# One written-out list of instructions in another order, on a kernel that runs attention and a feed-forward block on one core

## The chip, the cores and the metric

The kernel runs on one core of one Trainium2 chip. The metric is the device time of one execution in microseconds (us); lower is better. The engines are TensorE (PE, matmuls), VectorE (DVE), ScalarE (ACT), GpSimd (POOL) and SyncE (SP, which issues almost all transfers).

## The reference, cut to what matters

```
q, k, v: 8 batches x 8 heads x 576 rows x 64
q_s = softmax of q over its 64 columns;  k_s = softmax of k over its 576 rows
kv = k_s^T v  (64 x 64 per head);  x = q_s kv, laid out as 4608 tokens x 512
h = x @ w_in  (512 x 2048);  g = relu(h)^2;  out = g @ w_out  (2048 x 512)
```

The weights arrive as 64-bit floats (512 KB for each chunk of 128 hidden columns of w_in, and the same for w_out) and are taken apart into a high and a low fp32r half on the chip.

## The kernel before

**Blocks and words.** The tokens are worked in nine blocks: blocks 0 to 7 hold 512 tokens of one batch each, block 8 the 64 left over from every batch. A pair is two heads; a batch has four pairs. Every product of the feed-forward block is three fp32r matmuls (high x high, high x low, low x high).

The program is one text, `ORDER`, a list of 3969 words. Each word stands for the next step of one unit of work, and almost every step has instructions on a single engine. The loop at the end of the kernel walks the list once and emits each word's instructions; so the list fixes, for every engine, the order of its queue. Nothing reorders it later: an engine runs its own words strictly in the order of the list and waits wherever an input is not there yet.

**Words of the first phase** (pairs 0 to 7, block 0, and the weights). `Lq`, `Lk`, `Lv` load parts (a, b, ...) of q, k, v for a pair (all from SP's queue, but `Lk0b`, `Lq0b`, `Lq1a` and `Lq1b` from ACT's); `Wi`, `Wo` load a weight chunk. For a weight chunk: `wl` and `wt` (ACT) and `wc`, `wd` (DVE) build the fp32 value, through the fourth PSUM bank, `wh` (ACT) rounds it to the high half and `wp` (POOL) makes the low half. For a pair: `m`, `qm` (DVE maxima), `T`, `S` (PE, through which the largest k is spread), `mc`, `ks` (DVE), `ke`, `qe` (ACT, exponentials), `qs`, `qn` (POOL, subtract and scale q), `sm`, `rc` (DVE) with `sa` (POOL) between them, `vc` (POOL, copies v into place), `KV` (PE), `rs`, `kn` (scale kv), `TA`, `TB` (PE, turn q), `ca`, `cb` (ACT), `PX`, `PL` (PE, q times kv), `xh`, `xl` (split x). Block 0: `H` (PE, x times w_in), `r`, `sq`, `gh`, `gl`, `O` (PE). `Z` is a matmul of zeros on PE that computes nothing: a filler.

**Words of the later phase** have a colon and the number of the instance. `h1`, `r1`, `sq1`, `gh1`, `gl1`, `o0_1` to `o3_1` are block 1. From block 2 on two chunks of 128 hidden columns are made at a time by seven quarter products in place of eight: `B11`, `T1`, `T2`, `B21`, `B22`, `T3`, `T4`, each six matmuls of 256 columns, n = 0 to 55 counting the pairs of chunks over blocks 2 to 8. Between them stand short steps on the same PSUM banks: `seed` (ACT copies a bank after B11; T2 needs it), `e5` (ACT, after T1; B22 needs the bank), `u2` (ACT, after T2; T3 needs the bank), `a1` (DVE adds, after B22), `b1` (DVE adds, after T3; T4 needs the bank). Then `ra`/`rb`, `sqa`/`sqb`, `gha`/`ghb` (ACT) and `gla`/`glb` (DVE) make the squared activations, and `o0` to `o7` (PE, three matmuls of 512 columns each) multiply them with w_out; `away` stores a finished block.

The attention of later pairs runs beside it: `load_k`, `load_q`, `load_v` (SP), `k_max`, `k_less`, `k_bound`, `k_spread`, `q_max`, `q_less`, `q_sum`, `q_norm`, `q_turn` (DVE), `k_exp`, `q_exp`, `q_high`, `parts` (ACT), `q_low` (POOL), `kv` (PE and then DVE), `low0`, `low1`, `high` (PE, then ACT and DVE). `wo` and `s34` (SP) bring w_out and sums of w_in back from memory into rings of three tiles; `words`, `sums`, `s_high`, `s_low`, `ct..`, `cT..`, `cB..` prepare combinations.

**The two rings.** Passing tiles live in a ring of four (tag `raw`: sums, turned q, stored rows) and a ring of three (tag `w`: weight values; later three spare tiles). A new tile takes the place that has been held longest, and waits until its last user is done.

```
    with tc.manual_schedule():
        for token in ORDER:
            if ":" not in token:
                first_token(token)
                continue
            if token not in running:
                running[token] = units[token]()
            if isgenerator(running[token]):
                next(running[token], None)
```

Of the kernel before, what the change touches and what calls it, by code (L numbers as in the profile page):

```python
# [51 lines left out]
sm2 PL0@C0 Z PX0@B2 lf0 wli0 wci0 xh0 xl0 Z Z Z Z Z TB1@C0 T2@C1 mc2 Z Z Z TA1@B2 S2 cb1 wli1 KV1@C0 sa2 rc2 qn2 vc3
wdi0 ca1 wti1 ks2 rs1 wci1 Z TB2@C1 whi0 kn1 Lv2b Lk3b wpi0 Z Z PX1@C0 ke2 cb2 H0.0@B0 vc2 KV2@C1 TA2@B2 qm3 qs3 wdi1
xh1 whi1 wpi1 Lk3a Wi2 Lv4b m3 Wi3 Wo2 Wo3 Wi4 Lk4b Lq4b Lk5b Lq5b Lv5b Lq4a Wo0 Lk5a xl1 H0.1 rs2 kn2 wli2 wti2 ca2
PL1@B2 qe3 PL2@C1 lf2 lf1 wli3 wci2 PX2@C0 sm3 xh2 wdi2 sa3 rc3 qn3 xl2 H1.0@B1 T3@B2 H1.1 H1.2 mc3 wti3 whi2 wci3 wdi3
S3 TB3@C0 wpi2 H2.0@C2 H2.1 H2.2 wlo2 wlo3 ks3 wto2 whi3 wco2 wdo2 ke3 wpi3 wli4 wto3 cb3 KV3@B2 TA3@C1 rs3 kn3 who2
# [1105 lines left out]
```

## Time and profile before

| | before |
|---|---|
| three timed runs | 855.24, 855.8, 858.2 us; median 855.8 us |
| the profiled execution, its time | 855.73 us |
| its span, first to last instruction | 853.9 us |
| PE busy | 841.1 us (98% of the span) |
| DVE, ACT busy | 543.5 and 542.5 us (64% each) |
| POOL busy | 278.5 us (33%) |
| chain that ended last | PE 86%, DVE 4%, DMA 3%, ACT 3% |

The span is what the trace covers; 1.8 us of the execution's time lie around it. A busy time is the time in which at least one instruction of the engine is shown at work; for PE the ends of matmuls are modelled, and neighbours overlap, so busy does not mean that nothing is lost. The chain is followed back from the last instruction to whatever released it.

### The profile page before, as it was taken

Reading aid. Unit: us, or ns where it says so; the run is one execution under the profiler, and the core shown is the slowest. Engines: PE = TensorE matmul, PEld = TensorE weight load, DVE = VectorE, ACT = ScalarE, POOL = GpSimd, SP = SyncE. Lnnn points to the kernel's source line nnn. Section 1 sums busy time; section 2 is a strip of 40 time slices with the busy share of each in tenths; the row PEclk is TensorE's granted clock in tenths of the full one; section 3 lists DMA queues with packets and bytes.
Section 4 is the critical chain, followed back from the end, with each engine's and each line's share of the span. In section 5 each row is a group of like instructions: output and inputs, shape, how many; then the busy total and the mean of one; then the engine's idle time right before and its main releaser. Section 6 shows DMA issues by size and latency. Waiting matters only on the chain.

```text
span 853.9 us, 15149 instructions
## 1 busy us (share of the span) xinstructions
PE 841.1 (98%) x5377; PEld 735.7 (86%) x5377; DVE 543.5 (64%) x1077; ACT 542.5 (64%) x1102; POOL 278.5 (33%) x233
## 2 busy tenths in 40 slices
PE   8999999999999999999999999999999999999997
PEld 7688778888889898988988889888889898998996
DVE  7888878979896868577586768576843322322111
ACT  4998855567676776667666766677566544544433
POOL 4786842756534450222213221224112300210000
PEclk9999999999999999999999999999999999999999
DMA  9999745763886769666667487776846174443451
GB/s 219 288 311 269 221 127 171 254 213 94 255 247 177 229 188 280 197 222 186 196 184 251 141 217 233 222 213 168 238 126 230 37 242 145 161 157 127 141 180 50
DMA packets 121003, 166.68 MB, mean 195 GB/s; under 512 B 47584, under 2 KB 88544, under 8 KB 120928
## 3 DMA queue, kind: packets, MB, share of 16 engines
q1 hardware_dynamic: 120272, 165.03, 63.9%
q8 instruction: 42, 0.69, 0.4%
q10 hardware_dynamic: 656, 0.69, 0.3%
q14 instruction: 33, 0.27, 0.1%
HBM read 134.48 MB, written 31.20 MB: 194 GB/s over the span
## 4 chain that ended last, share of the span: by engine, by line
PE 86%; DVE 4%; DMA 3%; ACT 3%; SPq 2%; issue 1%; ACTq 0%; POOL 0%; DVEq 0%; POOLq 0%
PE bank L1076 30%; PE o_ps L727 14%; PE o_ps L729 14%; PE o_ps L728 14%; PE bank L710 3%; PE bank L712 3%; PE bank L711 3%; PE bank L695 2%; PE bank L622 1%; DMA wo<-out_kept 1%; DMA raw_i<-in_moe_w_in_dram 1%; DVE g_lo L721 1%; DMA qt<-in_q_dram 1%; DMA vt<-in_v_dram 0%; SPq L383 0%
## 5 line engine op out<-in xcount | busy, mean ns | idle before, releaser
L727 PE MATMUL o_ps<-wo,g_hi 128*128 128x512 f32 x576 | 228.0, 396 | 2.0 <-ACT g_hi L716 1.4
L729 PE MATMUL o_ps<-wo,g_lo 128*128 128x512 f32 x576 | 225.2, 391 | 0.2 <-DVE g_lo L721 0.2
L728 PE MATMUL o_ps<-wo,g_hi 128*128 128x512 f32 x576 | 224.9, 390 | 0.0
L721 DVE TENSOR_TENSOR g_lo<-r,g_hi 128x512 fp32r<-128x512 f32 x128 | 94.5, 741 | 105.4 <-ACT g_hi L716 104.8
L729 PEld LDWEIGHTS o_ps<-wo,g_lo 128*128 128x128 f32 x576 | 108.1, 188 | 25.3 <-DVE g_lo L721 1.4
L727 PEld LDWEIGHTS o_ps<-wo,g_hi 128*128 128x128 f32 x576 | 108.4, 188 | 23.0 <-ACT g_hi L716 1.8
L1037 ACT ACTIVATE r<-bank 128x512 f32<-128x512 f32 x128 | 76.5, 598 | 78.6 <-DVE bank L1094 43.3
L728 PEld LDWEIGHTS o_ps<-wo,g_hi 128*128 128x128 f32 x576 | 108.3, 188 | 19.4 <-issue 0.5
L716 ACT CAST g_hi<-r 128x512 fp32r<-128x512 f32 x128 | 79.1, 620 | 53.2 <-PE o_ps L728 49.4
L1076 PE MATMUL bank<-T,s 128*128 128x256 f32 x672 | 99.7, 284 | 0.2
L1076 PE MATMUL bank<-B,wi 128*128 128x256 f32 x672 | 99.0, 283 | 0.1
L618 POOL TENSOR_TENSOR q_hi<-qT,q_hi 64x640 fp32r<-64x640 f32 x24 | 39.3, 1636 | 178.6 <-ACT q_hi L613 125.9
L1076 PE MATMUL bank<-T,wi 128*128 128x256 f32 x672 | 96.1, 285 | 1.0 <-DVE bank L1096 1.0
L1076 PEld LDWEIGHTS bank<-T,wi 128*128 128x128 f32 x672 | 88.4, 190 | 5.3 <-DVE bank L1096 1.7
L1076 PEld LDWEIGHTS bank<-T,s 128*128 128x128 f32 x672 | 89.4, 190 | 3.7 <-ACT bank L1088 0.9
L1076 PEld LDWEIGHTS bank<-B,wi 128*128 128x128 f32 x672 | 89.3, 191 | 2.1 <-ACT bank L1088 0.9
L1042 ACT ACTIVATE r<-r 128x512 f32<-128x512 f32 x120 | 75.4, 631 | 2.0
L629 DVE TENSOR_TENSOR staged<-bank,corr 64x320 f32<-64x320 f32 (+1 forms) x96 | 42.9, 446 | 46.7 <-ACT corr L627 41.0
L434 POOL TENSOR_TENSOR B<-staged,B 128x512 fp32r<-128x512 f32 x21 | 28.6, 1364 | 118.1 <-ACT B L430 117.8
L1094 DVE TENSOR_TENSOR bank<-bank,spare 128x256 f32<-128x256 f32 x56 | 24.0, 428 | 56.9 <-PE bank L1076 41.8
L627 ACT COPY corr<-bank 64x320 f32<-64x320 f32 (+1 forms) x96 | 38.0, 396 | 33.0 <-PE bank L622 26.7
L1093 ACT COPY spare<-bank 128x256 f32<-128x256 f32 x56 | 20.9, 372 | 46.1 <-PE bank L1076 45.8
(193 smaller groups left out, 1398.7 us busy)
## 6 DMA issues: line engine op xcount, KB each, us to landing
wo<-out_kept SPq DMA_DIRECT2D x98, 512.0 KB, 4.5
s<-s_kept SPq DMA_DIRECT2D x53, 512.0 KB, 5.0
bounce<-tb SPq DMA_DIRECT2D x28, 320.0 KB, 4.3
qT<-bounce SPq DMA_DIRECT2D x104, 80.0 KB, 3.0
out_dram<-o SPq DMA_DIRECT2D x65, 128.0 KB, 2.9
raw_i<-in_moe_w_in_dram SPq DMA_DIRECT2D x16, 512.0 KB, 7.1
raw_o<-in_moe_w_out_dram SPq DMA_DIRECT2D x16, 512.0 KB, 6.9
out_kept<-wo SPq DMA_DIRECT2D x14, 512.0 KB, 3.8
```

The source lines that it names most:

```text
L434: nc.gpsimd.tensor_tensor(t[:, 1], src, t[:, 0].bitcast(F32), op=ALU.subtract)
L618: nc.gpsimd.tensor_tensor(st["q"][h][half[1 - h]], src, hi, op=ALU.subtract)
L627: nc.scalar.copy(corr, ps[HALF:])
L629: nc.vector.tensor_tensor(staged(b, pr // 2)[half[h], at : at + n], ps[:HALF], corr, op=ALU.add)
L716: nc.scalar.copy(g_hi, r)
L721: nc.vector.tensor_tensor(g_lo, r, g_hi.bitcast(F32), op=ALU.subtract)
L727: nc.tensor.matmul(acc, g_hi[:, ts], w[:, 0], start=(n == 0), stop=False)
L728: nc.tensor.matmul(acc, g_hi[:, ts], w[:, 1], start=False, stop=False)
L729: return nc.tensor.matmul(acc, g_lo[:, ts], w[:, 0], start=False, stop=(n == NFC - 1))
L1037: nc.scalar.activation(rs[key], ps, AF.Relu)
L1042: nc.scalar.activation(r, r, AF.Square)
L1076: nc.tensor.matmul(dst, lhs, rhs, start=start and c == n == 0, stop=c == 1 and n == 2, skip_group_check=True)
```

## The change

The list has the same words, but for two fillers: 47 `Z` in place of 49 (3967 words). They stand in another order on all engines, PE included. Steps of one unit keep their order among themselves. The two rings become seven places with names of their own: which place a new tile takes stands in the tables `RAW_AT` (69 tiles of the ring of four), `W_AT` (32 tiles of the ring of three) and `SPARE_AT`. The three tiles that the first phase holds in the ring of four get fixed places.

```
-RAWB, WB = 4, 3
...
+SPARE_AT = 1, 2, 0
+W_AT = "01201201201201201201201201201210"
+RAW_AT = "012301203123201121032031020320123021312032101130210323210231331200312"
...
+    raw_places = [0]
+
+    def raw_place(shape, name):
+        raw_places[0] += 1
+        return w_pool.tile(shape, F32, name=name, tag=f"raw{RAW_AT[raw_places[0] - 1]}", bufs=1)
...
-            t = temp["t1"] = w_pool.tile([P, 2 * QUAD], F32, name="t1", tag="raw", bufs=RAWB)
+            t = temp["t1"] = raw_place([P, 2 * QUAD], "t1")
...
-        qe = w_pool.tile([P, 4, LOW, BLK], F32, name="qe", tag="raw", bufs=RAWB)
-        left = w_pool.tile([P, 2 * NPAIR, LEFT], F32, name="left", tag="raw", bufs=RAWB)
-        tb = w_pool.tile([P, 4, LOW, BLK], F32, name="tb", tag="raw", bufs=RAWB)
+        qe = w_pool.tile([P, 4, LOW, BLK], F32, name="qe", tag="raw3", bufs=1)
+        left = w_pool.tile([P, 2 * NPAIR, LEFT], F32, name="left", tag="raw0", bufs=1)
+        tb = w_pool.tile([P, 4, LOW, BLK], F32, name="turning", tag="raw2", bufs=1)
...
-                w = w_of[part, fc] = w_pool.tile([P, 512], U32, name="w", bufs=WB)
+                w = w_of[part, fc] = w_pool.tile([P, 512], U32, name="w", tag=f"w{W_AT[len(w_of)]}", bufs=1)
...
-        spare.extend(w_pool.tile([P, 512], F32, name=f"spare{i}", tag="w", bufs=WB) for i in range(3))
+        spare.extend(w_pool.tile([P, 512], F32, name=f"spare{i}", tag=f"w{s}", bufs=1) for i, s in enumerate(SPARE_AT))
```

The list is too long to show. Its start, up to the fourth pair, with a run of Z written as one word here (Zx23), stands before as

```
Lq0a Lq0b qm0 qs0 Lk0b Lk0a m0 Zx23 T0@C0 Lk2a Lv0a Lk1a Lq1a Lq1b Lq2b Lv0b Lv3b Lk1b Lv3a Lq2a Lk2b Lq3a Wi0 Lv2a
Lv1a Lq3b Lv1b Wi1 qe0 sm0 mc0 sa0 rc0 qn0 vc0 qm1 Zx5 S0 ks0 ke0 Zx6 TB0@B2 TA0@C1 qs1 m1 qm2 KV0@C0 ca0 qe1 rs0 kn0
cb0 qs2 T1@C1 mc1 Zx3 S1 sm1 ks1 sa1 rc1 qn1 vc1 m2 qe2 ke1 wti0 sm2 PL0@C0 Z PX0@B2 lf0 wli0 wci0 xh0 xl0 Zx5 TB1@C0
T2@C1 mc2 Zx3 TA1@B2 S2 cb1 wli1 KV1@C0 sa2 rc2 qn2 vc3 wdi0 ca1 wti1 ks2 rs1 wci1 Z TB2@C1 whi0 kn1 Lv2b Lk3b wpi0
Zx2 PX1@C0 ke2 cb2 H0.0@B0 vc2 KV2@C1 TA2@B2 qm3 qs3 wdi1 xh1 whi1 wpi1 Lk3a Wi2 Lv4b m3 ... xl1 H0.1 rs2 kn2
```

and after as

```
Lq0a Lq0b qm0 qs0 Lk0a Lk0b Lq1b Lq1a m0 Zx23 T0@C0 mc0 Zx2 S0 Lq2b Lv0a Lv0b Lk1a Lk1b Lq2a Wi0 Lk2b Lk2a Lv2b Lv1b
Lv1a Wi1 Lk3a Lq3b Lk3b qe0 sm0 sa0 vc0 Lv2a Lq3a ks0 Wi2 rc0 qn0 qm1 ke0 Zx8 KV0@C0 TA0@C1 ca0 TB0@B2 m1 rs0 qm2 qs1
qs2 qe1 T1@C1 mc1 Zx2 S1 kn0 cb0 Zx2 PX0@B2 PL0@C0 wti0 qe2 lf0 xh0 wli0 sm1 ks1 sa1 rc1 qn1 m2 Zx4 T2@C1 ke1 sm2 xl0
mc2 TB1@C0 Z S2 Wi3 sa2 vc1 rc2 TA1@B2 cb1 ca1 qn2 KV1@C0 Z TA2@B2 wci0 wdi0 ks2 wli1 wti1 vc2 Wo2 Lv3a Lv3b Lv4d Wo3
rs1 ke2 kn1 whi0 ca2 wpi0 wci1 m3 wdi1 Zx2 TB2@C1 cb2 PX1@C0 PL1@B2 Z KV2@C1 H0.0@B0 qm3 lf1 xh1 whi1 T3@B2 wti2 wli2
qs3 qe3 wpi1 rs2 xl1 H0.1 kn2 mc3 wci2
```

Two places further on. Around T4:18 the list has before

```
... a1:18 T3:18 q_norm:14 parts:13 k_bound:7 k_spread:7 k_spread:7 b1:18 o0:18 o3:18 o2:18 o1:18 o4:18 o5:18 o7:18 o6:18
... ra:18 sqa:18 gha:18 q_high0:13 q_low0:13 q_high1:13 q_turn:14 T4:18
```

and after

```
... a1:18 sqb:17 ra:18 q_low0:13 parts:13 sqa:18 parts:13 parts:13 ghb:17 B11:19 T3:18 b1:18 glb:17 T1:19 T4:18
```

The list ends before with `o3:56 o7:56 away3:8 away3:8`, after with `away3:8 away3:8 o0:56 o4:56 away0:8 away0:8`.

## Rows read from the trace of the kernel before

**Rows 1.** The page's first lines: span, and each engine's busy time.

```profile
span 853.9 us, 15149 instructions
PE 841.1 (98%) x5377; PEld 735.7 (86%) x5377; DVE 543.5 (64%) x1077; ACT 542.5 (64%) x1102; POOL 278.5 (33%) x233
```

**Rows 2.** Busy time by stretches of 50 us: stretch, its length, then each engine.

```profile
core 0: us, PE busy (x) PEld busy (x) DVE busy (x) ACT busy (x) POOL busy (x), PEclk, DMA share, GB/s
0.00:50.00 50.00, 45.77 (x307) 36.66 (x308) 40.78 (x87) 35.71 (x71) 31.47 (x39) 1.00 0.98 262
...
800.00:854.00 54.00, 49.67 (x293) 43.86 (x291) 10.89 (x19) 21.54 (x43) 0.00 (x0) 1.00 0.32 111
sum 854.00, PE 841.10 PEld 735.67 DVE 543.48 ACT 542.49 POOL 278.51; mean PE 49.48 PEld 43.27 DVE 31.97 ACT 31.91 POOL 16.38
```

**Rows 3.** Who PE waited for, whole span: total us, times, longest us.

```profile
PE o_ps L727 <- ACT g_hi L716: 1.4, 1, 1.4
...
PE bank L1076 <- DVE bank L1096: 1.0, 1, 1.0
...
PE o_ps L727 <- DMA wo<-out_kept: 0.6, 1, 0.6
PE bank L622 <- DVE kf L703: 0.4, 1, 0.4
...
PE bank L695 <- DMA vt<-in_v_dram: 0.2, 1, 0.2
PE o_ps L729 <- DVE g_lo L721: 0.2, 1, 0.2
```

**Rows 4.** PE's timeline in the middle: start us, us, what.

```profile
230.00 0.88 PE L1076 MATMUL bank<-T,wi 128*128 128x256 f32 x6
230.98 0.98 PE L1076 MATMUL bank<-T,s 128*128 128x256 f32 x6
...
246.79 0.39 PE L728 MATMUL o_ps<-wo,g_hi 128*128 128x512 f32 x1
247.02 0.40 PE L729 MATMUL o_ps<-wo,g_lo 128*128 128x512 f32 x1
```

**Rows 5.** The page's groups: one 256-column product; busy, mean ns of one, idle.

```profile
L1076 PE MATMUL bank<-T,s 128*128 128x256 f32 x672 | 99.7, 284 | 0.2
```

**Rows 6.** PE's timeline in the head: KV1, H0.0, H4.0.

```profile
20.78 0.81 PE L836 MATMUL early<-vt,ke 128*64 128x65 f32 x20
...
24.71 0.79 PE L710 MATMUL bank<-x,wi 128*128 128x512 f32 x1
...
42.65 0.39 PE L710 MATMUL bank<-x,wi 128*128 128x512 f32 x1
```

**Rows 7.** DVE's timeline in the head: m1, rc2, ks2; in brackets the idle before.

```profile
12.15 1.28 DVE L792 TENSOR_REDUCE m<-kt 128x128 f32<-128x640 f32 x1 [1.08 <-DMA kt<-in_k_dram]
...
21.09 0.22 DVE L824 RECIPROCAL qs<-qs 128x10 f32<-128x10 f32 x1 [0.97 <-POOL qs L822]
...
21.77 0.81 DVE L806 TENSOR_TENSOR ke<-kt,early 128x640 f32<-128x640 f32 x1
```

**Rows 8.** POOL's timeline in the head: vc1.

```profile
20.00 0.72 POOL L838 COPY vt<-v_whole 128x640 f32<-128x640 f32 x1 [2.19 <-DMA v_whole<-in_v_dram]
```

**Rows 9.** ACT's timeline in the head: wli1.

```profile
21.73 0.68 ACT L906 ACTIVATE raw_i<-raw_i 128x512 uint32<-128x512 uint8 x1 [2.18 <-DMA raw_i<-in_moe_w_in_dram]
```

**Rows 10.** Transfers of the first 50 us together.

```profile
DMA packets 11335, 13.10 MB, mean 262 GB/s; under 512 B 1612, under 2 KB 10572, under 8 KB 11330
```

**Rows 11.** Who DVE waited for, 130 to 854 us: loads of k.

```profile
DVE spare L552 <- DMA kt<-in_k_dram: 2.4, 2, 1.7
```

**Rows 12.** ACT's timeline at the end: the last copy, after the last matmul.

```profile
849.70 0.59 ACT L746 COPY o<-o_ps 128x512 f32<-128x512 f32 x1 [0.73 <-PE o_ps L729]
```

**Rows 13.** Fillers alone in two early stretches: length, PE busy (count), granted clock.

```profile
1.00:4.00 3.00, 2.95 (x14) 2.96 (x15) 1.00 0.53 140
...
4.60:6.80 2.20, 2.20 (x22) 2.20 (x21) 1.00 1.04 230
```

More of the change, by code (lines that the diff above doesn't have):

```diff
@@ L52 @@
[L52 to L56, printed above, removed]
@@ L112 @@
-kv:2 away0:1 load_k:7 q_less:6 away1:1 gha:0 away2:1 low0:4 low0:4 away3:1 k_max:6 q_high1:4 q_low1:4 gla:0 rb:0 seed:1
-T2:1 u2:1 e5:1 sqb:0 ghb:0 B21:1 T3:1 B22:1 low1:4 a1:1 low1:4 ra:1 sqa:1 q_exp:6 o0:1 o3:1 o2:1 o1:1 gha:1 words:5
-words:5 q_back:5 away3:1 away1:1 low1:4 low1:4 load_v0:7 s34:2 load_v1:6 load_q:8 words:5 b1:1 high:4 q_max:7 sums:5
-sums:5 sums:5 B11:2 T4:1 T1:2 high:4 glb:0 rb:1 parts:5 parts:5 q_sum:6 q_sum:6 high:4 sums:5 e5:2 seed:2 gla:1
-q_norm:6 q_turn:6 high:4 high:4 parts:5 o4:1 o5:1 o6:1 o7:1 q_high0:5 sqb:1 ghb:1 s_high:5 q_less:7 o3:2 o1:2 q_low0:5
@@ L137 @@
-o0:8 cT4h:3 cT4l:3 q_low1:8 rb:7 kv:4 kv:4 kv:4 o3:8 o2:8 seed:8 parts:8 e5:8 parts:8 B22:8 sqb:7 B21:8 T2:8 ghb:7
-glb:7 parts:8 q_less:10 o6:8 o4:8 u2:8 a1:8 ra:8 sqa:8 away0:2 gha:8 T3:8 b1:8 T1:9 T4:8 B11:9 low0:8 o5:8 o7:8 q_out:9
-wo:15 s34:9 load_q:11 load_v0:11 away1:2 away2:2 away3:2 rb:8 seed:9 e5:9 B22:9 sqb:8 q_exp:10 q_sum:10 T2:9 B21:9
-ghb:8 low0:8 u2:9 T3:9 low0:8 gla:8 q_max:11 glb:8 k_max:10 a1:9 low1:8 low1:8 low1:8 q_sum:10 kv:4 b1:9 ra:9 q_back:9
-load_k:11 k_max:11 q_norm:10 k_bound:5 wo:16 o0:9 o2:9 o6:9 o1:9 o5:9 o4:9 o3:9 sqa:9 gha:9 gla:9 k_bound:5 k_spread:5
@@ L167 @@
-low0:12 sqb:16 ghb:16 o3:17 seed:17 glb:16 q_max:15 o4:17 T2:17 B21:17 u2:17 q_less:14 low0:12 q_exp:14 T3:17 b1:17
-a1:17 low1:12 low1:12 ra:17 sqa:17 gha:17 q_sum:14 low1:12 o5:17 o7:17 o6:17 away3:3 T4:17 high:12 B11:18 T1:18 rb:17
-high:12 seed:18 high:12 high:12 T2:18 e5:18 parts:13 sqb:17 q_back:13 load_q:16 s34:19 wo:31 q_sum:14 high:12 k_max:15
-gla:17 u2:18 ghb:17 glb:17 parts:13 B22:18 B21:18 k_bound:7 a1:18 T3:18 q_norm:14 parts:13 k_bound:7 k_spread:7
-k_spread:7 b1:18 o0:18 o3:18 o2:18 o1:18 o4:18 o5:18 o7:18 o6:18 away1:3 s34:20 load_v1:14 load_v1:15 low1:12
@@ L222 @@
-away2:5 away3:5 glb:32 u2:33 away0:5 T3:33 q_exp:22 low1:20 low1:20 b1:33 a1:33 load_k:23 o0:33 o1:33 o4:33 o2:33 o6:33
-o3:33 low1:20 away3:5 low1:20 away1:5 T4:33 ra:33 sqa:33 B11:34 rb:33 seed:34 T1:34 e5:34 q_sum:22 q_sum:22 q_norm:22
-q_turn:22 q_max:23 q_less:23 T2:34 B21:34 gha:33 gla:33 k_max:23 high:20 q_high0:21 k_bound:11 o5:33 o7:33 u2:34 sqb:33
-ghb:33 q_exp:23 B22:34 a1:34 ra:34 q_high1:21 glb:33 wo:59 wo:58 load_v0:22 wo:60 T3:34 o1:34 o0:34 o4:34 o2:34
-q_out:22 high:20 high:20 parts:21 parts:21 parts:21 high:20 high:20 b1:34 q_sum:23 k_bound:11 k_spread:11 o3:34 o7:34
@@ L272 @@
-o5:56 o4:56 o6:56 away0:8 away1:8 away1:8 away0:8 away2:8 away2:8 o3:56 o7:56 away3:8 away3:8
+Lq0a Lq0b qm0 qs0 Lk0a Lk0b Lq1b Lq1a m0 Z Z Z Z Z Z Z Z Z Z Z Z Z Z Z Z Z Z Z Z Z Z Z T0@C0 mc0 Z Z S0 Lq2b Lv0a Lv0b
+Lk1a Lk1b Lq2a Wi0 Lk2b Lk2a Lv2b Lv1b Lv1a Wi1 Lk3a Lq3b Lk3b qe0 sm0 sa0 vc0 Lv2a Lq3a ks0 Wi2 rc0 qn0 qm1 ke0 Z Z Z
+Z Z Z Z Z KV0@C0 TA0@C1 ca0 TB0@B2 m1 rs0 qm2 qs1 qs2 qe1 T1@C1 mc1 Z Z S1 kn0 cb0 Z Z PX0@B2 PL0@C0 wti0 qe2 lf0 xh0
+wli0 sm1 ks1 sa1 rc1 qn1 m2 Z Z Z Z T2@C1 ke1 sm2 xl0 mc2 TB1@C0 Z S2 Wi3 sa2 vc1 rc2 TA1@B2 cb1 ca1 qn2 KV1@C0 Z
@@ new lines @@
+rb:0 sqb:0 seed:1 gla:0 q_max:7 o7:0 low1:4 low1:4 away3:1 o0:1 B22:1 ghb:0 T2:1 u2:1 high:4 B21:1 T3:1 q_less:6 glb:0
+high:4 parts:5 sums:5 sums:5 b1:1 q_exp:6 q_high0:5 q_sum:6 a1:1 ra:1 o1:1 o2:1 o6:1 o3:1 o7:1 o4:1 load_k:7 away3:1
+q_sum:6 parts:5 q_norm:6 high:4 parts:5 sqa:1 gha:1 high:4 q_turn:6 q_less:7 high:4 gla:1 sums:5 load_v1:6 away1:1
+s34:3 low1:4 wo:3 load_v1:7 T1:2 T4:1 B11:2 e5:2 B22:2 q_low0:5 k_max:7 sums:5 rb:1 seed:2 T2:2 u2:2 q_exp:7 sqb:1
+q_high1:5 s_high:5 o3:2 o5:1 B21:2 low0:5 low0:5 o1:2 o2:2 T3:2 q_low1:5 words:5 a1:2 low0:5 low1:5 o0:2 ghb:1 glb:1
@@ new lines @@
+parts:7 gla:4 q_max:9 q_less:9 sums:7 u2:5 high:6 high:6 T3:5 parts:7 b1:5 a1:5 cB11h:3 q_exp:9 q_high0:7 ct1:3 o2:5
+o0:5 o3:5 o1:5 T4:5 ra:5 s_high:7 ghb:4 high:6 sqa:5 gha:5 high:6 glb:4 rb:5 sqb:5 B11:6 k_max:9 k_bound:4 q_sum:9
+s_high:7 k_bound:4 q_low0:7 load_v1:8 q_out:8 seed:6 low1:6 q_high1:7 T1:6 low0:7 wo:10 s_low:6 cT1l:3 s_low:7 cB11l:3
+q_low1:7 s_low:7 o7:5 o4:5 o6:5 o5:5 e5:6 low0:7 s_low:7 low0:7 T2:6 u2:6 B21:6 B22:6 gla:5 T3:6 q_max:10 a1:6 low1:7
+o0:6 o2:6 o3:6 o1:6 ghb:5 glb:5 b1:6 ra:6 sqa:6 T4:6 B11:7 low1:7 low1:7 k_spread:4 cB21h:3 rb:6 seed:7 T1:7 T2:7 e5:7
@@ new lines @@
+q_high1:8 q_low0:8 q_low1:8 kv:4 wo:16 load_v0:11 glb:7 q_sum:10 a1:8 o3:8 b1:8 kv:4 kv:4 kv:4 o4:8 kv:4 parts:8
+parts:8 away0:2 ra:8 parts:8 load_k:11 wo:14 wo:15 q_back:9 s34:11 T1:9 T4:8 low0:8 o6:8 o5:8 low0:8 low0:8 away1:2
+low1:8 o7:8 sqa:8 low1:8 e5:9 q_sum:10 away3:2 low1:8 B11:9 rb:8 seed:9 away2:2 gha:8 B22:9 T2:9 high:8 u2:9 B21:9 T3:9
+parts:9 parts:9 sqb:8 gla:8 k_max:11 away2:2 q_high0:9 ghb:8 a1:9 parts:9 q_norm:10 glb:8 o0:9 o1:9 o2:9 o3:9 o4:9 o5:9
+high:8 away0:2 away3:2 wo:17 q_high1:9 q_low1:9 q_low0:9 high:8 b1:9 T4:9 ra:9 high:8 sqa:9 gha:9 k_bound:5 q_max:11
@@ new lines @@
+rb:12 seed:13 low1:10 low1:10 o6:12 o1:12 o0:12 low1:10 load_v1:12 low1:10 load_v1:13 wo:22 load_q:15 wo:23 B22:13
+T2:13 sqa:12 u2:13 gha:12 B21:13 gla:12 a1:13 ra:13 sqa:13 high:10 sqb:12 k_max:12 T3:13 o7:12 o4:12 b1:13 q_sum:13
+q_sum:13 B11:14 T1:14 T4:13 o3:13 o5:12 q_high0:11 high:10 high:10 ghb:12 high:10 parts:11 parts:11 o1:13 o2:13 o0:13
+gha:13 e5:14 k_max:13 k_bound:6 glb:12 q_high1:11 o4:13 o6:13 o5:13 o7:13 q_out:12 load_q:14 q_low0:11 rb:13 seed:14
+sqb:13 ghb:13 T2:14 u2:14 B21:14 B22:14 high:10 parts:11 q_max:14 gla:13 k_bound:6 k_spread:6 T3:14 low0:11 wo:24
@@ new lines @@
+low0:12 q_back:13 b1:17 ra:17 o7:16 sqa:17 away3:3 o0:17 o3:17 ghb:16 o1:17 o2:17 gha:17 s34:20 q_exp:15 low0:12
+low1:12 low1:12 k_max:15 T1:18 B11:18 low1:12 T4:17 high:12 high:12 glb:16 rb:17 q_high0:13 q_high1:13 high:12 high:12
+e5:18 seed:18 gla:17 o4:17 o7:17 o6:17 o5:17 o2:18 B21:18 B22:18 T2:18 o0:18 o3:18 o1:18 low1:12 wo:31 k_bound:7
+k_bound:7 k_spread:7 k_spread:7 high:12 u2:18 a1:18 sqb:17 ra:18 q_low0:13 parts:13 sqa:18 parts:13 parts:13 ghb:17
+B11:19 T3:18 b1:18 glb:17 T1:19 T4:18 low0:13 o6:18 o4:18 q_low1:13 gha:18 low0:13 k_less:14 low0:13 low1:13 e5:19
@@ new lines @@
+B11:25 b1:24 parts:16 T4:24 T1:25 low0:16 glb:23 rb:24 o6:24 o4:24 o5:24 k_max:18 away1:4 e5:25 seed:25 low0:16 low0:16
+gla:24 away2:4 q_exp:18 o7:24 sqb:24 ghb:24 away0:4 glb:24 B21:25 T2:25 low1:16 load_k:19 load_v0:19 s34:25 s34:26
+low1:16 low1:16 away3:4 o0:25 o2:25 o6:25 o3:25 o7:25 o4:25 o1:25 away3:4 low1:16 away0:4 away1:4 s34:27 wo:45 u2:25
+B22:25 k_max:19 k_bound:9 a1:25 ra:25 high:16 T3:25 T1:26 B11:26 b1:25 T4:25 o5:25 high:16 sqa:25 gha:25 gla:25 o3:26
+high:16 q_sum:18 wo:46 o0:26 rb:25 seed:26 parts:17 parts:17 q_high0:17 o2:26 o1:26 wo:47 load_q:20 q_sum:18 parts:17
@@ new lines @@
+glb:32 away3:5 b1:33 load_v0:22 load_v1:22 q_back:21 away0:5 o0:33 o2:33 o6:33 high:20 k_max:22 high:20 o1:33 o3:33
+ra:33 parts:21 q_high0:21 q_high1:21 parts:21 q_turn:22 k_bound:11 k_bound:11 k_spread:11 T4:33 B11:34 q_low0:21
+low0:21 rb:33 sqb:33 low0:21 sqa:33 o4:33 o5:33 o7:33 seed:34 T2:34 u2:34 T1:34 B21:34 e5:34 gha:33 gla:33 B22:34
+low1:20 load_v1:23 wo:58 low0:21 a1:34 ra:34 sqa:34 ghb:33 wo:59 load_v0:23 T3:34 q_low1:21 q_out:22 s34:36 away3:5
+away1:5 away2:5 wo:60 q_back:22 s34:37 k_spread:11 b1:34 o2:34 o1:34 o3:34 T4:34 B11:35 low1:21 glb:33 o6:34 o0:34
```

391 lines of the change are left out of this document (189 added, 202 removed).

## The prediction

> **What bounds the kernel now.** I read the busy times first, then their course in stretches, then PE's waits, and last the timelines of the head. PE is shown at work for 841.1 us of a span of 853.9 us, DVE and ACT for 64% of it [rows 1]. So the end is set by PE, and the order can only change what PE loses: 853.9 - 841.1 = 12.8 us of idle time, and what is hidden inside the busy time. The stretches say where the idle time lies: 50 - 45.77 = 4.2 us in the first 50 us, 54 - 49.67 = 4.3 us in the last (almost all of it after the last matmul), and the other 12.8 - 4.2 - 4.3 = 4.3 us between [rows 2]. In the middle six waits are named: 1.4 + 1.0 + 0.6 + 0.4 + 0.2 + 0.2 = 3.8 us [rows 3]. They cost more than this: a 512-column matmul is shown as 0.39 us long while the next begins after 0.23 us [rows 4], so each wait is about 0.39 - 0.23 = 0.16 us longer than the gap in the record. Six times 0.16 is 1.0 us. And a wait can vanish in the record altogether: the six matmuls that begin at 230.00 are over after 0.88 us and one lasts 0.28, so they begin (0.88 - 0.28) / 5 = 0.12 us apart and take the engine for 6 x 0.12 = 0.72 us, yet the next group begins after 0.98 us, 0.26 us late [rows 4, 5]; it is a T2 behind its `seed`. I found three such, 0.8 us together. What PE loses in the middle is then 3.8 + 1.0 + 0.8 = 5.6 us. The rest of the middle is matmuls back to back.
>
> **The change, part by part.**
>
> *PE's work.* The words are the same, so the matmuls are: no term. Two fillers go, four matmuls of zeros, in the head, where PE waits anyway: nothing, and at most 4 x 0.10 = 0.4 us if they stood in the way [rows 13].
>
> *The places of the rings.* A table instead of a turn adds no instruction. It changes which old user a new tile waits for, and this is part of the order: no term of its own.
>
> *The tail.* PE's last word is now o4:56, followed by away0, one copy on ACT and one transfer from SP; before it was o7:56 and away3, one copy of 0.59 us [rows 12] and a transfer in two halves on two queues. Same copy, same bytes: 0, with 0.3 us either way for the one queue.
>
> *The head.* Three loads hold engines up: k of pair 1 holds DVE for 1.08 us before `m1`; v of pair 1 holds POOL for 2.19 us before `vc1`, and as `sa2` stands behind `vc1` DVE's `rc2` waits 0.97 us more; the second chunk of w_in holds ACT for 2.18 us before `wli1` [rows 7 to 9]. In the first 50 us transfers move 262 GB/s [rows 10], by which a part of 128 to 160 KB takes 0.5 to 0.6 us, and they land in the order of the queue. In SP's queue Lk1b moves from place 9 to 7, the last part of v1 from 18 to 14 and Wi1 from 19 to 15, so they land about 1.2, 2.4 and 2.4 us sooner; and `sa2` now stands ahead of `vc1`. I then went down the queues word by word with the durations of the timelines. `m1` can begin when sm0, ks0, rc0 and qm1, now all ahead of it, are done, at 11.5 in place of 12.15; `rc2` waits no more; so `ks2` comes at 20.4 in place of 21.77 [rows 7]. On POOL `vc1` comes at 18.4 in place of 20.00 [rows 8] and KV1 on PE at 19.2 in place of 20.78 [rows 6]: 1.6 us. Further on this shrinks, because ACT and DVE have hardly a pause from 22 to 43 us and the first chunk of w_in is only 0.3 us earlier at PE: it stands behind `ke2` and `kn1` in ACT's queue now. H0.0 in the new order has KV2, TA2 and PL1 before it; counted by the same words, H4.0 comes at about 41.8 where it began at 42.65 [rows 6]. So the head gives 0.9 us. The bounds are 0 (ACT's queue eats all of it) and the 1.6 us of KV1. The transfers that are pushed back for this are q and v of pairs 2 and 3 (Lq3a from place 13 to 20, Lv3a and Lv3b to 24 and 25); their users, qm3 and vc3, come at 24 and after 32 us, when by the same 0.6 us a part and 2 us a weight chunk they have landed at about 21.5 and 27.
>
> The TensorE's fillers are there for its clock. The granted clock is 1.00, the level of 2.4 GHz, in every row; but fourteen fillers take 3.0 us at the start and twenty-two take 2.2 us from 4.6 us on, 0.21 against 0.10 us each, after 3.5 us of unbroken work [rows 13]. The Trainium skill, TensorE: Matmul & The Clock Gate, Part 1: The HAM clock gate, states that the clock's normal state is the throttled one, at half rate, and that an idle engine falls back to it. The trace agrees with the first half, by the two lengths of a filler; that idle time brings it back no row here shows, since the longest gap of the head is 0.8 us. It would speak against thinner fillers, and is a rival below.
>
> *The middle.* Each of the nine losses has a kind, and I sized the new ones by how each kind is covered in the two lists. A copy or a sum between two matmul words is tight when the PE work between source and user, at 0.12 us for 256 columns and 0.23 for 512, leaves it less than 0.3 us. Counted so, tight places fall from 68 to 50: `b1` from 16 to 6, `u2` from 25 to 19, `e5` from 12 to 9, `seed` from 15 to 16.
> - `b1` to T4 (L1096): 1.0 idle, 1.2 with the overlap. At T4:18 the 13 parts, k_bound and k_spread stood ahead of `b1` on DVE; after, only `glb` follows it and none of these lies between T3:18 and T4:18. By 6/16 of the tight places: 0.45.
> - `gha`/`gla` to `o` (L716, L721): 1.4 and 0.2 idle, 1.9 with the overlap. The thinnest margin of a whole chain falls from 1.2 to 0.8 us for `gla` and grows from 1.1 to 2.3 for `glb`. I take half, 0.95.
> - `kf` to low0 (L703): 0.4, 0.55 with the overlap; the margins are alike: 0.55.
> - Loads of w_out and v: 0.6 and 0.2, 1.15 with the overlap. A v part is now never freed by SP's queue less than 10.8 us of PE work before its `kv` (before, 3.5); for w_out the shortest is 4.8 us in both. Half: 0.6.
> - `seed` to T2: 0.8, by 16/15: 0.85.
> Together 0.45 + 0.95 + 0.55 + 0.6 + 0.85 = 3.4 us in place of 5.6: a gain of 2.2. The bounds: all of it gone, 5.6; or as much more lost as is lost now by the two kinds that did not get better (`kf`, `seed`) and by loads that come later (below), 1.4 + 2.4 = 3.8 us worse.
>
> *Sum.* 855.73 us of the profiled execution (1.8 us around its span; it stands 0.07 us under the median of 855.8, so I don't shift it) - 0.9 - 2.2 = 852.6 us.
>
> **The rivals.** About 0.3%, 2.6 us, is what a measurement of this kernel can tell from no change: 853.2 and 858.4 are the borders.
>
> *As many waits, elsewhere.* The old list has nine losses in 800 us, none of which its order was asked to have; a list of the same words may have as many, at other places. For it: 50 tight places are still many, and some chains now stand thinner, as B22:25 to o3:26, five steps over ACT and DVE with 0.8 us to spare. Against it: DVE and ACT are two thirds busy [rows 1], so one late word is caught up soon. Then only the head is left, and half of it at that: 855.7 - 0.5 = 855.2 us.
>
> *Later loads of k and q, slower.* SP's order now has loads closer to their first use: listed less than 4 us of PE work ahead of k_max or q_max are 12, before 6. SP runs ahead of the list as long as nothing holds it, which is why so few show: in the old trace DVE waited for k twice, 2.4 us together, the longest 1.7 [rows 11]. With twice as many such places DVE would wait 4.8 us, and behind k_max in its queue stand `a1`, `b1` and `gla`, for which PE waits. It decides where a wait is longer than what PE has before the next T1 or T4, mostly 1 to 3 us. If each of the extra waits and half of the old ones come through, PE loses 2.4 + 1.2 = 3.6 us more, and the nine losses stay: 855.7 + 3.6 - 0.5 = 858.8 us.
>
> *The clock falls in the head.* In the new list PE has two fillers before S0 and S1 where it had five and three, and gaps of about 0.4 us. If its clock went to 1.2 GHz there, KV1 would take 1.62 us for 0.81 [rows 6]. Some ten real words lie between 9 and 24 us, none longer than about 1 us, so PE would lose up to 8 us, of which fillers and waits of that stretch hide most; I take 2: 857.7 us. The gaps are no longer than those that cost nothing now, so I hold it unlikely.
>
> *It does nothing to PE* is the first rival without the head: 855.7.
>
> **How the numbers follow.** The forecast, fewer waits and an earlier head, 850 to 853.2: 0.46. As many waits elsewhere (or none of it), 853.2 to 858.4: 0.40, the clock's 0.02 among them. Later loads or another bad place, above 858.4: 0.14. So faster by over 0.3% 0.46, within 0.40, slower 0.14. The likeliest one's own range is 850 to 853.2 us. For 8 in 10: the low end takes all losses of the middle and the head's bound, 855.7 - 5.6 - 1.6 = 848.5, of which I cut half a us, 849.0, as all nine gone and none new is rare; the high end reaches into the slower case, to 857.8.
>
> **What would show it.** Head: `m1`'s and `rc2`'s idle gone, KV1 near 19.2, H4.0 near 41.8, and PE's idle time in the first 50 us not above 4.2. Middle: PE's named waits after 50 us well under 3.8 us, the one on L1096 gone. Wrong, if DVE's waits for DMA of kt or qt grow beyond 2.4 us with PE waiting for L1094 or L1096 right after; or if H4.0 stands at 42.6 or later; or if matmuls of the head take twice their time.

## The result, and the profile after

| | before | after |
|---|---|---|
| median of four runs each | 855.82 us | 848.17 us (846.33 to 849.5) |
| ratio, 95% interval | | 0.9904 (0.9877 to 0.9931) |
| the profiled execution | 855.73 us, span 853.9 | 847.74 us, span 845.1 |

So it is faster by 1.0%, well beyond the 0.3% that a measurement can tell. The forecast was 852.6 us: the direction held, the time lies 0.8 us under the range.

The page's first lines after, to set against [rows 1]:

```profile
span 845.1 us, 15154 instructions
PE 836.7 (99%) x5373; PEld 734.3 (87%) x5373; DVE 552.6 (65%) x1077; ACT 541.1 (64%) x1102; POOL 279.4 (33%) x233
```

PE does the same matmuls but for four of zeros (at most 0.4 us by [rows 13]), yet its busy time falls by 841.1 - 836.7 = 4.4 us. So half of the 8.8 us of span was inside the time shown as busy. The Trainium skill, Perfetto Trace Analysis, Identifying the Most-Contended Engine, warns that the share of matmul busy time does not tell how close a kernel is to its limit, because matmuls are pipelined. These two profiles agree that it does not, by those 4.4 us; but the page has pipelined instructions look smaller in the trace, while here a 512-column matmul is shown as 0.39 us long and the next begins after 0.23 us [rows 4], so that the busy time hides idle time.

The stretches of 50 us after, against [rows 2]; one with a named wait each at 350 and 600:

```profile
core 0: us, PE busy (x) PEld busy (x) DVE busy (x) ACT busy (x) POOL busy (x), PEclk, DMA share, GB/s
0.00:50.00 50.00, 46.94 (x310) 37.66 (x311) 40.44 (x87) 36.82 (x73) 31.46 (x39) 1.00 0.92 249
...
350.00:400.00 50.00, 49.20 (x340) 43.82 (x339) 33.76 (x62) 32.25 (x67) 11.67 (x8) 1.00 0.67 188
...
600.00:650.00 50.00, 49.37 (x340) 44.16 (x339) 26.59 (x58) 30.45 (x64) 8.83 (x6) 1.00 0.62 190
```

The first 50 us are idle for 3.1 us in place of 4.2. The waits of PE after, against [rows 3]:

```profile
PE early L970 <- DVE zeros L359: 1.0, 1, 1.0
PE o_ps L736 <- DMA wo<-out_kept: 0.8, 2, 0.6
PE bank L890 <- ACT qT L871: 0.6, 1, 0.6
PE bank L1085 <- DVE bank L1103: 0.6, 1, 0.6
PE early L890 <- ACT kvn L860: 0.6, 2, 0.4
PE early L809 <- DVE mc L807: 0.4, 2, 0.2
PE bank L720 <- DVE x L899: 0.3, 1, 0.3
```

Those on `early`, L890 and L720 are of the head. The middle has two kinds left: loads of w_out (0.8) and `a1` before T1:16 (0.6); 1.4 us stand against 3.8. The waits for `g_hi` and `kf` and that of T4:18 (L1096 there) are gone. At T4:18 twelve matmuls, T1:19 and T4:18, now run through:

```profile
426.74 0.88 PE L1085 MATMUL bank<-T,s 128*128 128x256 f32 x6
427.46 1.67 PE L1085 MATMUL bank<-T,wi 128*128 128x256 f32 x12
```

The head after, from the timelines of PE, DVE, POOL and ACT, against [rows 6 to 9]: KV1 and H4.0; `m1`, `rc2`, `ks2`; `vc1`; `wli1`. None has idle time before it.

```profile
18.79 0.80 PE L845 MATMUL early<-vt,ke 128*64 128x65 f32 x20
...
41.05 0.39 PE L719 MATMUL bank<-x,wi 128*128 128x512 f32 x1
...
10.87 1.28 DVE L801 TENSOR_REDUCE m<-kt 128x128 f32<-128x640 f32 x1
...
18.04 0.20 DVE L833 RECIPROCAL qs<-qs 128x10 f32<-128x10 f32 x1
...
19.47 0.81 DVE L815 TENSOR_TENSOR ke<-kt,early 128x640 f32<-128x640 f32 x1
...
17.71 0.72 POOL L847 COPY vt<-v_whole 128x640 f32<-128x640 f32 x1
...
19.01 0.71 ACT L915 ACTIVATE raw_i<-raw_i 128x512 uint32<-128x512 uint8 x1
```

**Where the 8.0 us came from.** I set both traces side by side by a lag: the time minus the matmul work begun until then, at 0.12 us for a matmul of 256 columns and 0.227 for one of 512, the spacing of unbroken work. Its level depends on the price given to the few other shapes; the differences between lists hardly do. At 43 us the lag is 23.2 before and 21.6 after; at 835 us 42.9 and 34.7. So the head gives 1.6 us and the middle (42.9 - 23.2) - (34.7 - 21.6) = 6.6 us. From the last matmul's start to the end of the span it is 4.7 us before and 4.1 after, a gain of 0.6; around the span 1.8 and 2.6, 0.8 us worse. Together 1.6 + 6.6 + 0.6 - 0.8 = 8.0 us.

**What a wait costs that the record hardly shows.** PE's weight loads around the T2 of [rows 4], before:

```profile
229.88 0.79 PEld L1076 LDWEIGHTS bank<-T,wi 128*128 128x128 f32 x6
230.98 0.77 PEld L1076 LDWEIGHTS bank<-T,s 128*128 128x128 f32 x6 [0.31 <-ACT bank L1088]
```

The T1 whose matmuls begin at 230.00 has its first weights loaded from 229.88 on, ahead of them. The T2 that waits for its `seed` loads at 230.98, when its first matmul begins: nothing was loaded ahead. And its six matmuls last 0.98 us in place of 0.88 [rows 4]: the second matmul comes 0.22 us behind the first and not 0.12. I call a word a late start when its first weight load begins less than about 0.10 us ahead of its matmul, in place of 0.12 or more. It costs its own delay (the time by which its first matmul comes later than the spacing of unbroken work), and more at its second matmul: 0.10 us where nothing was loaded ahead, less where part of the load was. The Trainium skill, TensorE: Matmul & The Clock Gate, Part 2: What happens when you issue a matmul, says that weight loads are pulled ahead of running matmuls; the trace agrees, by 0.12 us in the first row, and shows that a waiting word loses this.

Counted over the words from 43 us on (without `kv`, whose matmuls have 65 columns), before has 94 late starts (own delays 7.5 us, second matmuls 5.6 us), after 70 (2.9 and 3.6). Their difference, 13.1 - 6.5 = 6.6 us, is as large as the gain of the middle. Another execution of the list of after has 7.2 us for 6.5 (after_again, below), so these sums hold to within about 0.7 us.

### The profile page after: what moved, and what is told of

Its sections match the earlier page's. It is cut to its first block, busy times and chain, and to the rows that moved or that the text cites. A ratio compares the mean times of both kernels' runs of the same rounds, so it can differ in the third digit from the quotient of the medians.

```text
span 845.1 us, 15154 instructions
## 1 busy us (share of the span) xinstructions
PE 836.7 (99%) x5373; PEld 734.3 (87%) x5373; DVE 552.6 (65%) x1077; ACT 541.1 (64%) x1102; POOL 279.4 (33%) x233
## 4 chain that ended last, share of the span: by engine, by line
PE 87%; DVE 4%; DMA 3%; ACT 2%; SPq 1%; issue 1%; ACTq 0%
PE bank L1085 32%; PE o_ps L736 14%; PE o_ps L737 14%; PE o_ps L738 14%; PE bank L719 3%; PE bank L721 3%; PE bank L720 3%; PE bank L704 2%; PE bank L631 1%; DMA wo<-out_kept 1%; DMA raw_i<-in_moe_w_in_dram 1%; DMA qt<-in_q_dram 1%; DVE g_lo L730 1%; SPq L751 1%; DMA kt<-in_k_dram 1%
## 5 line engine op out<-in xcount | busy, mean ns | idle before, releaser
L638 DVE TENSOR_TENSOR staged<-bank,corr 64x320 f32<-64x320 f32 (+1 forms) x96 | 42.9, 447 | 43.7 <-ACT corr L636 42.3
L443 POOL TENSOR_TENSOR T<-staged,T 128x512 fp32r<-128x512 f32 x21 | 27.9, 1341 | 78.7 <-ACT T L439 74.5
```

The source lines that it names most:

```text
L443: nc.gpsimd.tensor_tensor(t[:, 1], src, t[:, 0].bitcast(F32), op=ALU.subtract)
L638: nc.vector.tensor_tensor(staged(b, pr // 2)[half[h], at : at + n], ps[:HALF], corr, op=ALU.add)
```

## The experiments

Each is a list of the same words, but for the two fillers. Rows of the traces are set against the same account: late starts from 43 us on, and by how much the lag grows from 43 to 835 us.

| list | late starts | own delay | second matmul | lag grows | span | ratio to before |
|---|---|---|---|---|---|---|
| before | 94 | 7.5 | 5.6 | 19.7 | 853.9 | 1 |
| after | 70 | 2.9 | 3.6 | 13.1 | 845.1 | 0.9904 |
| after_again | 73 | 3.4 | 3.8 | 13.5 | 846.2 | 0.9911 |
| rings_turn | 67 | 2.2 | 3.4 | 11.9 | 844.7 | 0.9914 |
| e2 | 76 | 3.6 | 4.1 | 14.6 | 847.3 | 0.9933 |
| e1b | 93 | 7.6 | 5.7 | 20.6 | 853.4 | 1.0028 |
| e9 | 97 | 8.3 | 5.9 | 21.5 | 854.2 | 0.9990 |
| e3 | 93 | 3.9 | 5.5 | 15.5 | 850.4 | 0.9954 |
| e3b | 86 | 6.5 | 4.8 | 18.1 | 852.8 | 0.9986 |
| e5 | 72 | 2.0 | 3.7 | 12.8 | 844.7 | 0.9903 |
| e5b | 65 | 4.1 | 3.0 | 13.7 | 846.9 | 0.9929 |
| e4 | 79 | 14.9 | 5.3 | 26.1 | 859.0 | 1.0080 |

A line through the twelve, lag growth against own delay plus second matmul, has the slope 0.98 and leaves no list more than 0.7 us off, with 6.8 us that every list loses otherwise. With the own delay alone the slope is 1.16 and lists lie up to 1.6 us off. So both parts are needed. This is bookkeeping and not a test of cause: the delays are parts of the lag that they are set against. What it shows is that the rest is alike in all lists, within 0.7 us; whether a wait that is put in or taken out moves the end is tested by e4 and e3. The list e1 is not in the table, as its clock fell for a while (below).

**Which part of the list: e1, e2, e1b.** Head and middle of the two lists were exchanged, with the ring places worked out anew.

```
e1:  after up to H4.0, then before        e2:  before up to H4.0, then after
e1b: after up to words:5 ... low0:4 (228 us), then before
```

> The list of after up to H4.0 (its first 41 us), the list of before from there on; ring places worked out anew. The theory is that PE sets the end, so that each wait of PE that goes stays gone and the pieces add up: head -1.6 us, middle -6.7 us. Then this kernel gains only the head: 855.8 - 1.6 = 854.2 us, H4.0 at 41.1 and the last matmul 1.6 us sooner than before. The rival, that the head's gain is eaten later by waits that were hidden: 855.8, with the lead of 1.6 us at 43 us shrinking in the middle.

Measured: 861.05 us, ratio 1.0045 (1.0027 to 1.0063). The expectation failed at the seam, and twice. The two fillers that the new head has no use for stand in this list just ahead of H4.0 on PE; they wait for DVE, H4.0 comes at 42.66 and not at 41.1, and the head's lead is gone there already. The row of PE's waits for them:

```profile
PE early L969 <- DVE r L950: 0.7, 1, 0.7
```

The second loss is at H6.0. PE's timeline:

```profile
59.94 0.39 PE L737 MATMUL o_ps<-wo,g_lo 128*128 128x512 f32 x1
62.79 0.47 PE L718 MATMUL bank<-x,wi 128*128 128x512 f32 x1 [2.46 <-DVE ke L814]
...
64.50 0.63 PE L720 MATMUL bank<-x,wi 128*128 128x512 f32 x1
```

and two stretches of it, with the granted clock ahead of the last two columns:

```profile
60.50:62.70 2.20, 0.00 (x0) 0.00 (x0) 2.14 (x4) 2.05 (x5) 1.29 (x2) 1.00 1.04 395
...
64.20:66.20 2.00, 2.00 (x6) 1.42 (x5) 2.00 (x4) 2.00 (x5) 1.64 (x3) 0.50 1.12 293
```

H6.0 waits 2.46 us for DVE's `ks`, which in the mixed list stands behind weight steps that after had put elsewhere. Behind the wait the granted clock is 0.50 for some 3 us, the level of 1.2 GHz, and matmuls of 512 columns begin 0.43 us apart. The lag grows by 4.7 us between 60 and 70 us (before: 0.5). Behind that, o4:35 waits 1.53 us and T4:18 1.21, as in before. So e1 does not tell what the new head would bring by itself; it shows that a head cut off at 41 us leaves work to the words behind it, which the old order does not do in time.

> The list of before up to H4.0, the list of after from there on. If the pieces add up: 848.2 + 1.6 = 849.8 us, H4.0 at 42.7 and about 13 us lost by PE from there on, as in after. If the middle of after needs the earlier head (its loads and splits come sooner), more waits show up behind 43 us and it ends above 851.

Measured: 851.18 us, ratio 0.9933 (0.9916 to 0.9949), which is 0.9933 x 855.8 = 850.1 us on the scale of the expectation's 849.8. The new middle alone brings some 5.7 of the 7.7 us, and stands without the new head.

> The list of after for the first 228 us, from there on that of before; the seam lies where the two have worked the same words but for four, so that no wait comes from the seam itself. Up to there after is ahead by about 1.8 us in the trace (1.6 of them in the head). If the pieces add up: 1.8 us under before, a ratio of 0.998, and behind the seam the waits of before one for one (o4:35 1.5 us, T4:18 1.2, o5:2 0.8). If the gain of the early part is lost later: ratio 1.000.

Measured: ratio 1.0028 (1.0011 to 1.0044); the span of its profiled execution is 853.4 us, 0.5 under before, and the waits of before came back one for one (o4:35 1.53 us, T4:18 1.21). The lead at 43 us of 1.4 us had shrunk to 0.5 at 835. So neither forecast holds by the median. The twelve timed runs lie from 854.1 to 861.0 us; the four longest have a mean granted clock of 0.995 to 0.998, the other eight of 0.998 to 1.000. No trace shows where those lost it; why this list loses it oftener stays open.

**The tables: rings_turn.** The source of before, which takes the places by turns, with the list of after.

```
-            t = temp["t1"] = raw_place([P, 2 * QUAD], "t1")
+            t = temp["t1"] = w_pool.tile([P, 2 * QUAD], F32, name="t1", tag="raw", bufs=RAWB)
...
-                w = w_of[part, fc] = w_pool.tile([P, 512], U32, name="w", tag=f"w{W_AT[len(w_of)]}", bufs=1)
+                w = w_of[part, fc] = w_pool.tile([P, 512], U32, name="w", bufs=WB)
```

> The list of after, but the two rings by turns as in before, without the tables. If the order alone makes the gain: 848.2 us, within 1. If the tables carry a part of it, a new tile by turns waits for a later user, DVE or SP is held, PE waits behind it: 850 to 856.

Measured: 850.01 us, ratio 0.9914 (0.9895 to 0.9933), span 844.7. The 850.01 us must not be set against the rival's 850: before took 857.3 us beside it, and on the scale of the expectation it is 0.9914 x 855.8 = 848.4 us. The tables carry no part of the gain that can be measured; the order does.

**The head's loads alone: e9.** Words of SP's queue, then of POOL, PE and DVE:

```
-Lk2a Lv0a Lk1a Lq2b Lv0b Lv3b Lk1b Lv3a ...     +Lq2b Lv0a Lv0b Lk1a Lk1b Lq2a Wi0 Lk2b ...
-vc1 ... KV1@C0 sa2 rc2 qn2 vc3                  +sa2 vc1 KV1@C0 rc2 qn2 ... Lv3a Lv3b vc3
```

> The list of before with the first 22 loads of SP in the order of after, sa2 ahead of vc1 and KV1, and vc3 behind its loads; all else as before. By the prediction the waits of m1 (1.08 us), vc1 (2.19), rc2 (0.97) and wli1 (2.18) go, KV1 starts at about 19.2 us in place of 20.8, and H4.0 0.9 us sooner, within 0 to 1.6: a ratio of 0.999. If the head's gain comes from the new order of PE, ACT and DVE instead: KV1 and the waits are better, H4.0 where it was (42.6, give or take 0.7 us that executions of one list differ by).

Measured: ratio 0.9990 (0.9979 to 1.0001). From the timelines of POOL and PE:

```profile
17.42 0.73 POOL L846 COPY vt<-v_whole 128x640 f32<-128x640 f32 x1
...
19.37 0.80 PE L844 MATMUL early<-vt,ke 128*64 128x65 f32 x20
...
41.05 0.39 PE L718 MATMUL bank<-x,wi 128*128 128x512 f32 x1
...
58.73 0.47 PE L718 MATMUL bank<-x,wi 128*128 128x512 f32 x1 [0.27 <-DVE ke L814]
```

The loads do nearly all that the prediction said of them (KV1 at 19.37 for 19.2), and H4.0 comes 1.6 us sooner. But by 70 us the lag is 24.0, where before has 23.8: late starts at H5.0 (0.36 us, for POOL's low half of a weight), H6.0 (0.43, for DVE's `ks`) and O4.1 (0.22) are among what gives it back. The interval of the ratio reaches 1, so a gain over the whole run is not shown. In after the lead at 70 us is still 23.8 - 22.4 = 1.4 us.

**Nine long waits covered in the old list: e3, e3b.**

```
-T3:18 q_norm:14 parts:13 k_bound:7 k_spread:7 k_spread:7 b1:18
+T3:18 b1:18 q_norm:14 parts:13 k_bound:7 k_spread:7 k_spread:7
-o0:35 o4:35 ra:35 ... o2:35 o3:35 o7:35 o1:35 o6:35
+o0:35 ra:35 ... o2:35 o3:35 o7:35 o1:35 o4:35 o6:35
```

> The list of before with only the nine longest waits of its middle covered by local moves (b1:18 straight behind T3:18; another matmul word put between the source and the waiting word for o4:35, o5:2, low0:18, o0:30, T2:1, T2:32, B21:39 and kv:2). Their delays are 1.53 + 1.20 + 0.79 + 0.56 + 0.42 + 0.37 + 0.30 + 0.27 + 0.26 = 5.7 us, and each costs about 0.1 us more, as the second matmul of a word that begins late comes 0.1 us late too: 6.5 us. If waits that go stay gone: 855.8 - 6.5 = 849.3 us, 849.3 to 850.3 with a wait or two come back. The rival, that in a list so full a wait comes back at the next place: 853.5 or more.

Measured: 852.47 us, ratio 0.9954 (0.9936 to 0.9971): 3.9 us gained, 851.9 us on the scale of the expectation, between the two. Seven of the nine waits are gone, T4:18 and o4:35 among them. Two were only handed on, as B21:1 and B21:32 stand in the place of T2 and need the same `seed` (0.25 and 0.26 us). Of the 5.2 us of own delay removed (0.4 of them at kv:2, which the table leaves out), 5.2 - 0.4 - (7.5 - 3.9) = 1.2 came back at new places, the longest 0.30 us at T4:39.

> The list with the nine long waits covered, and on top of it thirteen moves of one word each for the waits of 0.12 to 0.30 us that are left there (B11:40 ahead of T4:39, o5:31 ahead of B21:32, and so on). Together 2.6 us of delay and 1.2 us of late second matmuls, 3.8. If small waits count as long ones do, and as large a share stays gone as with the nine (4.2 of 6.5): 2.5 us more, a ratio to before of 0.9925. If all stays gone: 0.991, nearly that of after by moves of 22 places in the old list. If small waits are no loss, or all come back: 0.9955, as without the thirteen.

Measured: ratio 0.9986 (0.9975 to 0.9996), worse than e3. Its moves removed most of the small waits and set up long ones: the row of PE's waits that leads is

```profile
PE o_ps L737 <- DVE g_lo L729: 1.6, 1, 1.6
```

as o1:3, drawn ahead of T2:3, now comes before its `gla:2`; B11:40 waits 1.1 us, B22:14 0.9, T4:35 0.7. All three forecasts missed. So it does not tell whether small waits can be covered one by one; that they count follows from the account alone.

**Waits put in: e4.** For sixteen pairs of chunks in the last third:

```
-T2:43 ... u2:43 ... T3:43          +T2:43 u2:43 T3:43 ...
```

> The list of after, but for 16 pairs of chunks between n = 39 and 55 T3 stands straight behind T2, the other matmul words of that place behind it: PE then waits for u2 sixteen times. In after T3 comes just in time with one word of 0.72 us between, so each should wait about 0.7 us. If PE sets the end and each late start costs 0.1 us on its second matmul: 16 x (0.7 + 0.1) = 12.8 us over after. If only the wait counts: 11.2 us. If waits in this stretch, where DVE and ACT are a third busy, are caught up later: under 6 us. If the clock falls behind such short waits: far more than 13.

Measured: 862.27 us, ratio 1.0080 (1.0066 to 1.0093), which is 1.008 - 0.990 = 1.8% or 15 us over after; by the spans 859.0 - 845.1 = 13.9 us. PE's timeline at T2:43 and T3:43, and then the row of its waits:

```profile
699.51 0.93 PE L1084 MATMUL bank<-T,s 128*128 128x256 f32 x6
700.89 0.97 PE L1084 MATMUL bank<-T,s 128*128 128x256 f32 x6 [0.46 <-ACT spare L1101]
```

```profile
PE bank L1084 <- ACT spare L1101: 7.4, 16, 0.5
```

Each shows 0.46 us of idle time; its own delay is 0.62 us (0.46 and the 0.16 by which the matmul ahead is shown too long), and its second matmul comes 0.10 us late. 16 x 0.72 = 11.5 us; T1:47 and T1:49 now wait 0.74 and 0.75 us too. All late starts together have grown by (14.9 + 5.3) - (2.9 + 3.6) = 13.7 us, by own delays alone 12.0; the span grew by 13.9. The timed runs of one list lie up to 4 us apart, so this alone does not decide between 13.7 and 12.0. It does rule out that such waits are caught up later (under 6 us): nothing was, though DVE and ACT have ample time there, and the clock stayed at 1.00.

**More out of after: e5, e5b, after_again.**

```
e5:  -s34:36 away3:5 away1:5 away2:5 wo:60     +wo:60 s34:36 away3:5 away1:5 away2:5
     -q_less:14 k_less:13 ... a1:15            +a1:15 q_less:14 k_less:13
e5b: -B11:19 T3:18 b1:18                       +T3:18 B11:19 b1:18
     -k_bound:7 k_bound:7 k_spread:7 k_spread:7 high:12 u2:18 a1:18
     +a1:18 k_bound:7 k_bound:7 k_spread:7 k_spread:7 high:12     (and u2:18 ahead of o3:18)
```

> The list of after with six of its remaining waits covered by local moves (wo:60 sent ahead of three stores and wo:23 ahead of load_q:15, for o3:35 and o4:13; a1:15 ahead of q_less:14 and k_less:13, for T1:16; o0:18 ahead of B21:18; o0:36 ahead of T2:37; B21:15 ahead of T2:15). Their delays are 0.75 + 0.75 + 0.33 + 0.23 + 0.20 + 0.20 = 2.5 us, with 0.1 for each late start 3.1. The nine waits that were covered in the list of before gave 4.2 of 6.5 us in the trace, as smaller waits came up behind them. By that share: 3.1 x 4.2 / 6.5 = 2.0 us under after, a ratio to before of 0.988. If nothing new comes up: 0.987. If the list is so full that each comes back: 0.990, as after.

> The list of after with the six moves and some fifteen more for the waits that came up behind them or were left (0.59 us at low1:22, 0.38 at B11:19, and ten of 0.02 to 0.20): 2.1 us of delay and 1.3 us of late second matmuls, 3.4. Of the first six moves about a third stayed gone: 1.1 us under after, a ratio of 0.989. If all stays gone: 0.9863. If all comes back: 0.990, as after.

> The kernel after once more, beside the two others on one chip: ratio 0.990, and late starts from 43 us on of 6.5 us by the trace.

Measured: e5 0.9903 (0.9890 to 0.9916), e5b 0.9929 (0.9913 to 0.9945), after_again 0.9911 (0.9894 to 0.9928). Five of e5's six covers held, and low1:22 (0.59 us) and B11:19 (0.38) came up behind them. e5b came out slower than any of its forecasts. There I had drawn `a1:18` ahead of k_bound and k_spread on DVE; it stands there until `u2:18` is done, they come after it, `b1:18` after them, and T4:18 waits. DVE's timeline at `a1:18` and PE's at T4:18:

```profile
423.81 0.43 DVE L1102 TENSOR_TENSOR bank<-bank,spare 128x256 f32<-128x256 f32 x1 [5.26 <-ACT spare L1101]
...
428.88 0.98 PE L1084 MATMUL bank<-T,wi 128*128 128x256 f32 x6 [1.98 <-DVE bank L1104]
```

So no version beats after by what can be measured.

## Why the prediction was right and wrong

**Right: what bounds it, PE's work, the tables.** The end is set by PE and moves with what PE loses (e4: 13.7 us put in, 13.9 out). The tables are no term (rings_turn).

**The head was under-sized: 0.9 taken, 1.6 measured.** Its steps held with something to spare: `m1` 10.87 for 11.5, `ks2` 19.47 for 20.4, `vc1` 17.71 for 18.4, KV1 18.79 for 19.2. The step "Further on this shrinks" was the wrong one: H4.0 came at 41.05, the bound of 1.6 and not 41.8. Executions with one head differ here: H4.0 lies at 41.7 to 43.3 in four with the old head (mean 42.7) and at 40.9 to 41.8 in seven with the new (mean 41.3; without e1, where the fillers stand in the way), so 1.4 us is the better figure. What I did not see is that this gain has a price behind 43 us, which e9 pays and after does not.

**The failed step: what the middle loses.** "The rest of the middle is matmuls back to back" was false. I had counted the nine long waits, 5.6 us; they measure 5.7, of which 0.4 (kv:2, for the load of v) stands outside the count of late starts. The late starts cost 13.1 us: 5.3 for the other eight, and what I had put at nothing, the second matmuls of all 94, 5.6 us, and some ten waits of 0.10 to 0.20 us with smaller ones, 2.2 us. With less than half of the loss in sight, the gain came out as 2.2 in place of 6.6 us; and the part in sight was under-sized too, 2.2 for 3.0. Split in the same way, the gain is: waits over 0.21 us 5.3 to 2.3 (3.0 us), smaller ones 2.2 to 0.65 (1.6), second matmuls 5.6 to 3.6 (2.0).

**The kinds** (own delay and second matmul, before and after; in brackets what I forecast, without second matmuls): T4 behind `b1` 2.5 and 0.5 us (1.2 and 0.45); `o`, for g and for loads, 3.4 and 1.3; low0 1.6 and 0.2 (0.55, no change); T2 behind `seed` 1.3 and 1.2 (0.8, no change). `b1` and `seed` went the way their tight places said (16 to 6, 15 to 16); `kf` did not, as I had only compared margins. T3, B22, B21 and T1, which I had given nothing, cost 3.8 before and 2.7 after.

**The rivals.** As many waits elsewhere: no, 70 late starts with 2.9 us for 94 with 7.5. Later loads of k and q: they did come later, DVE's waits for them from 130 us on are

```profile
DVE spare L561 <- DMA kt<-in_k_dram: 1.8, 2, 1.5
DVE qm L573 <- DMA qt<-in_q_dram: 1.5, 1, 1.5
```

3.3 us in place of 2.4 [rows 11]. But no word of PE starts late within the five us behind the long ones (at 373.7 and 497.7 us): the wait at T1:16 (at 392.5) has `a1` behind two steps of DVE's own. The clock in the head: it did not fall, with fewer fillers. KV1 takes 0.80 us for 0.81. PEclk reads 1.00 throughout, but it reads so over the first slow fillers of [rows 13] too: the trace's record of the clock begins only behind them, at 4.6 us before and 4.9 after, so there the length of a filler is the better sign.

**Tail.** 0 forecast; 0.6 us gained behind the last matmul and 0.8 lost around the span, which in other executions of the new list is 2.0 to 2.9 us, so no more can be said.

**What stays open.** Why the new order has so few small waits was not shown edit by edit: covering the nine long ones of the old list by hand gave 3.9 us of the 8, and set up others. That the second matmuls and the small waits cost the end what the account says was not tested by an edit of its own. And some 6.8 us of the growing lag belong to no late start in any list; a part of them is only the price given to the other shapes.
